# Giving every product with the transposed probabilities one stationary shape, 128 columns and 128 rows

## The chip, the cores and the metric

The kernel runs on one core of a Trainium2 chip. Its time is the device time of one launch in microseconds; three runs of the kernel before took 1256.52, 1258.52 and 1259.30 us, so the median is 1258.52. A profile is one further execution. The engines are TensorE (PE in the profile; its weight loads are a row of their own, PEld), VectorE (DVE), ScalarE (ACT), GpSimd (POOL), and SyncE (SP), whose queue issues all DMAs of this kernel.

## The reference

For 8 batches and 8 heads of 576 positions with 64 features, causal attention with a decay bias is computed, and its output goes through a feed-forward network (FFN) with an ELU:

```python
scores = scale * np.matmul(q, k.transpose(0, 1, 3, 2))
cum = np.cumsum(np.maximum(s, 0.0), axis=-1)
bias = -(cum[:, :, :, None] - cum[:, :, None, :])
scores = np.where(causal, -1000000000.0, scores + np.minimum(bias, 0.0))
attn = np.exp(scores - np.max(scores, axis=-1, keepdims=True))
attn = attn / (np.sum(attn, axis=-1, keepdims=True) + 1e-09)
out = np.matmul(attn, v)
# then, with x the 4608 x 512 matrix of all heads' outputs:
h = x @ w_in                                   # 512 x 2048
g = np.where(h > 0.0, h, np.exp(np.minimum(h, 0.0)) - 1.0)
y = g @ w_out                                  # 2048 x 512
```

All inputs and the output are float32.

## The kernel before

**Units.** Attention is worked through in 96 units, three for each of the 8 x 4 pairs of heads: one "pair" unit for the first 64 queries of both heads (`h is None`), and one unit for each head (`h` 0 and 1) with the other 512 queries. Each unit loads its operands (`prepare`), makes scores, softmax and scaled probabilities (`scoring`), and multiplies them with the values (`weighing`). The steps of one unit's weighing are interleaved with the scoring of the next.

**Two ways of arithmetic.** The first 24 units are "native": f32 operands, probabilities turned on TensorE (line 848) and copied out of PSUM into a tile `pc` (`split_pt`). In the units behind them a head's probabilities are split into an f16 high and low part (`halved`) and turned by transposing DMAs into a tile `T` (line 751). There are 48 such units. Their values are split too: three parts, each the upper 16 bits of a float32 word, lie in the tile `vs` as `[128, 5, 3, 64]`: five blocks of 128 keys, three parts, 64 features. `values` loads the tile and makes parts 1 and 2 by subtraction on POOL or DVE (line 660).

**The products.** For each key block `kb` of a head's unit `keys` (line 836) issues, into one PSUM bank `av`, a product of the first two parts side by side (128 stationary columns) with the high half of the probabilities, one of the third part (64 columns) with the high half, and one of the first two parts with the low half. The moving operand has 512, 448, 320 and 192 columns for blocks 0 to 3. The last block has 64 keys; its high and low halves share the 128 rows, so there are two products, the third part's with 64 rows and 64 columns. That makes 14 products for a unit, all of line 815. `halves` then adds the upper and the lower 64 rows of the result together.

**Buffers.** `vs` has two places, taken in turn by all three kinds of unit. `pc` has two places of 512 words, used by native head units and by the pair units. `T` has two places (`N_T`), one of which first holds the decay sums (`aux`, line 381).

**The FFN.** It runs in 12 chunks of 384 rows of x. A chunk has 16 steps `f`: 12 products of line 955 into `h`, the ELU on ACT, DVE and POOL, and 9 products of line 979 into `o`. Attention's outputs reach it through DRAM (`x_dram`).

**What sets the order.** Every operation is recorded with its engine (or several to choose from), a duration assumed by hand, its priority and the tiles it reads and writes. `Plan.issue` then places them greedily: of all operations that are ready and have a buffer, the one with the earliest start goes next, and the order on each engine is fixed so. A product with the transposed probabilities is assumed to take 0.4525 ns per moving column, whatever its stationary shape. A change in a buffer's number of places therefore may move instructions anywhere in the program.

Of the kernel before, what the change touches and what calls it, by code (L numbers as in the profile page):

```python
# [9 lines left out]
F32 = mybir.dt.float32  # L10
F32R = mybir.dt.float32r
# [6 lines left out]
P = 128  # L18
# [222 lines left out]
def pe4(n):  # L241

    return 4 * pe(n)
# [36 lines left out]
def kernel(  # L280
# [91 lines left out]
    k2 = [plan.buf(const, [P, S], F32R, f"k2_{k}") for k in range(2)]  # L372

    WM = S - P
    maskw = plan.buf(const, [P, WM], BF16, "maskw")
    masks = plan.buf(const, [P, 2, HB], BF16, "masks")

# [26 lines left out]
    def ones():  # L404

        for q, k in ((q2s, k2s), *zip(q2, k2)):
            def rows(q=q, k=k):
                pool.memset(q.v[HB:].bitcast(F32), 1.0)
                pool.memset(k.v[HB:].bitcast(F32), 0.0)

            op(-8, [("Pool", 700.0, rows)], [], [(q, "ones"), (k, ("aux", 0)), (k, ("aux", 1))])

    def mask_tiles():
        def whole():
# [129 lines left out]
    def prepare(u):  # L544

        b, j, h, prio = u.b, u.j, u.h, u.prio
        dt = F32 if u.native else F32R
        direct = u.native and (b, j) == (0, 0)
        u.vs = plan.buf(sb, [P, NQ + 1, 3, D], F32R if h is None and not u.native else F32,
                        f"vs_{u.tag}", tag="vs", bufs=2)  # L550
        if h is None:
            w, n, m = P, 2 * HB, 1
            u.qs = plan.buf(sb, [P, NQ * P], dt, f"qs_{u.tag}", tag="qs", bufs=2)
            u.kh = plan.buf(sb, [P, 2, HB], dt, f"khs_{u.tag}", tag="khs")
            u.q2, u.k2 = q2s, k2s
            heads = slice(2 * j, 2 * j + 2)

            def q_src():
                return qT[b, j, :, :P]

            def k_src():
                return kT[b, :, heads, :HB]

            def v_src():
                return vb[b, j, :, 0:1]

            def aux_src(m):
                h0 = b * H + 2 * j
                if direct:
                    return aux.v[h0 : h0 + 2, 0, :HB]  # L570
                return aux_dram.v[h0 : h0 + 2, m, :HB]

            def q_view(t):
                return t

            def k_view(t):
                return t.rearrange("p (h t) -> p h t", h=2)

            def k_own(t, rows):
                return t.v[rows]  # L580
        else:
            w, n, m = P * NQ, S, 1 + NQ
            u.qs = plan.buf(sb, [P, NQ * P], dt, f"qs_{u.tag}", tag="qs", bufs=2)
            spare = u.native and u.turn
            u.kh = plan.buf(sb, [P, S], dt, f"kh_{u.tag}", tag="st" if spare else "kh",
                            bufs=N_ST if spare else N_K)
            u.q2, u.k2 = q2[u.turn], k2[u.turn]
            hh = 2 * j + h

            def q_src():  # L590
                own = qT[b, j, :, P:].rearrange("p (i h t) -> p i h t", h=2, t=P)
                return own[:, :, h]

            def k_src():
                return kT[b, :, hh, :n]

            def v_src():
                return vb[b, j, :, 1:].rearrange("p (i h) d -> p i h d", h=2)[:, :m, h]

            def aux_src(m):  # L600
                h0 = b * H + hh
                return aux.v[h0 : h0 + 1, 0, :n] if direct else aux_dram.v[h0 : h0 + 1, m, :n]

            def q_view(t):
                return t.rearrange("p (i t) -> p i t", t=P)

            def k_view(t):
                return t

            def k_own(t, rows):  # L610
                return t.v[rows, :n]
        if u.native:

            load(prio, lambda: k_own(u.kh, slice(0, HB)), lambda: k_src()[:HB], [],
                 [(u.kh, "k")], HB * n * 4)
            at = slice(HB, HB + 1)
            op(prio, [("Pool", pool_1(w), lambda: pool.memset(u.qs.v[at, :w], 1.0))], [], [(u.qs, "ones")])
            load(prio, lambda: k_own(u.kh, at), lambda: aux_src(0),
                 [(aux, 0) if direct else (aux_dram, 0)], [(u.kh, "aux")], n * 4)
            load(prio, lambda: q_view(u.qs.v[:HB, :w]), lambda: q_src()[:HB], [],  # L620
                 [(u.qs, "q")], HB * w * 4)
            values(u, prio, v_src, m)
            return
        st = st_buf(f"stk_{u.tag}")
        load(prio, lambda: k_view(st.v[:, :n]), k_src, [], [st], P * n * 4)
        for m_ in range(2):
            at = slice(HB + 32 * m_, HB + 32 * m_ + 1)
            load(prio, lambda m_=m_, at=at: k_own(u.k2, at).bitcast(F32), lambda m_=m_: aux_src(1 + m_),
                 [(aux_dram, 1 + m_)], [(u.k2, ("aux", m_))], n * 4)
        sq = st_buf(f"stq_{u.tag}")  # L630
        load(prio, lambda: q_view(sq.v[:, :w]), q_src, [], [sq], P * w * 4)
        rounded(prio, w, lambda: u.qs.v[:, :w], lambda: sq.v[:, :w], [sq], [(u.qs, 0)])
        load(prio, lambda: u.q2.v[:HB, :w].bitcast(F32),
             lambda: u.qs.v[:HB, :w].bitcast(F32), [(u.qs, 0)], [(u.q2, "q")], HB * w * 4)
        rounded(prio, n, lambda: k_own(u.kh, slice(0, P)), lambda: k_view(st.v[:, :n]), [st], [u.kh])
        rest(prio, w, lambda: u.qs.v[HB:, :w], lambda: sq.v[HB:, :w],
             lambda: u.qs.v[HB:, :w].bitcast(F32), [sq, (u.qs, 0)], [(u.qs, 1)])
        rest(prio, n, lambda: k_own(u.k2, slice(0, HB)), lambda: k_view(st.v[:HB, :n]),
             lambda: k_own(u.kh, slice(0, HB)).bitcast(F32), [st, u.kh], [(u.k2, "kl")])
        if h is not None:  # L640
            values(u, prio, v_src, m)
            return
        sv = st_buf(f"stv_{u.tag}")

        def v3():
            return sv.v[:, :D].rearrange("p (n d) -> p n d", d=D)

        load(prio, v3, v_src, [], [sv], P * D * 4)
        rounded(prio, D, lambda: u.vs.v[:, :1, 0], v3, [sv], [u.vs])
        rest(prio, D, lambda: u.vs.v[:, :1, 1], v3,  # L650
             lambda: u.vs.v[:, :1, 0].bitcast(F32), [sv], [u.vs])
# [98 lines left out]
            ], [sm, (pt, "pad"), (t16, high)], [(t16, low), (pt, "data")])  # L750
        turned_load(prio, units[i], lambda: u.pt.v[:, (i + 1) % NQ :: NQ][:, : units[i]], lambda: t16.v, [t16], [(u.pt, i)])

    def split_pt(prio, tag, native, tr, w, t0=0, rows=P):
        pc = plan.buf(sb, [P, 512], F32 if native else F32R, f"pc_{tag}", tag="pc", bufs=2)
        psum_copy(prio, w, lambda: pc.v[:rows, :w], lambda: tr.v[:rows, t0 : t0 + w], [tr], [(pc, 0)])
        if native:
            return [(pc, 0)]
        op(prio, [("DVE", dve_p(w), lambda: dve.tensor_tensor(
            pc.v[:, 256 : 256 + w], tr.v[:, t0 : t0 + w], pc.v[:, :w].bitcast(F32), ALU.subtract))],
           [tr, (pc, 0)], [(pc, 1)])  # L760
        return [(pc, 0), (pc, 1)]

# [44 lines left out]
    def weighing(u):  # L807
# [11 lines left out]
        if u.h is None:  # L819
            def pair():  # L820
# [5 lines left out]
                products(pe4(P) if u.whole else pe(P), [  # L826
                    ([pc, u.vs], lambda pc=pc, m=m: (
                        u.vs.v.rearrange("p n a d -> p n (a d)")[:, 0, :rows],
                        pc[0].v[:, 256 * m : 256 * m + P]), rows)
                    for m, pc in enumerate(pieces)], slice(P), True, True)  # L830
                for h in range(2):
                    halves(prio, u.whole, 1.0, h, HB, u.x_part((h, 0)), 0, av, h * HB)
# [3 lines left out]
        def keys(kb):  # L836
# [3 lines left out]
            if u.whole:  # L840
# [3 lines left out]
                def turned():  # L844

                    ks = slice(kb * P, kb * P + rows)
                    for n, i in enumerate(range(i0, NQ)):
                        pe_.transpose(tr.v[:rows, n * P : (n + 1) * P], u.pp[i].v[:, ks], ident)

                op(prio, [("PE", 111.0 * (NQ - i0), turned)], [u.pp[i] for i in range(i0, NQ)], [tr])  # L850
                pc, = split_pt(prio, f"{u.tag}_{kb}", True, tr, c, HB * half, rows)
                products(pe4(c), [([pc, u.vs], lambda: (u.vs.v[:rows, kb, 0], pc[0].v[:rows, :c]), HB)],
                         dst, kb == 0, kb == NQ)
            else:

                i0 = max(kb - 1, 0)

                def part(m, rows):
                    if kb == NQ:
                        return u.pt.v[:rows, 0, P - c :]  # L860
                    end = (1 + (2 * kb + m + 1) * NQ) * P
                    return u.pt.v.rearrange("p u q -> p (u q)")[:rows, end - c : end]

                def two():
                    return upper(u.vs.v.rearrange("p n a d -> p n (a d)"))[:, kb, : 2 * D]

                def third(rows):
                    return upper(u.vs.v)[:rows, kb, 2]

                used = [(u.pt, i) for i in range(i0, NQ)]  # L870
                two_parts, three_parts = [(u.vs, 0), (u.vs, 1)], [(u.vs, 2)]
                rows = HB if kb == NQ else P
                pairs = [(used + two_parts, lambda m=m: (two(), part(m, P)), P)
                         for m in range(1 + (kb < NQ))]
                pairs.insert(1 - kb // NQ, (used + three_parts, lambda: (third(rows), part(0, rows)), HB))
                products(pe(c), pairs, dst, kb == 0, kb == NQ)
            if kb == NQ:
                halves(prio, u.whole, 1.0 if u.whole else 1.0 / UP, u.h, P * NQ,
# [211 lines left out]
```

## Time and profile before

| | us |
|---|---|
| median of three runs | 1258.52 |
| the profiled execution | 1260.03 |
| its span, first to last instruction | 1258.1 |
| PE busy | 1207.2 |
| POOL busy | 820.5 |
| DVE busy | 728.2 |
| ACT busy | 656.5 |
| granted TensorE clock, mean | 0.989 of full |

A row of the profile that names a line and an engine tells the operation, then what it writes and reads (`av<-T,vs`); for a PE row, `128*64` is the stationary operand's rows and columns and `128x512 f16` the moving operand. Matmuls are pipelined, so the durations of neighbours overlap, and the distance between two starts tells what one of them costs. In the views of waits, a row reads: engine and line that waited, `<-` whom it waited for, us in total, times, longest.

### The profile page before, as it was taken

Reading aid. Unit: us, or ns where it says so; the run is one execution under the profiler, and the core shown is the slowest. Engines: PE = TensorE matmul, PEld = TensorE weight load, DVE = VectorE, ACT = ScalarE, POOL = GpSimd, SP = SyncE. Lnnn points to the kernel's source line nnn. Section 1 sums busy time; section 2 is a strip of 40 time slices with the busy share of each in tenths; the row PEclk is TensorE's granted clock in tenths of the full one; section 3 lists DMA queues with packets and bytes.
Section 4 is the critical chain, followed back from the end, with each engine's and each line's share of the span. In section 5 each row is a group of like instructions: output and inputs, shape, how many; then the busy total and the mean of one; then the engine's idle time right before and its main releaser. Section 6 shows DMA issues by size and latency. Waiting matters only on the chain.

```text
span 1258.1 us, 19717 instructions
## 1 busy us (share of the span) xinstructions
PE 1207.2 (96%) x5888; PEld 935.4 (74%) x5888; DVE 728.2 (58%) x1849; ACT 656.5 (52%) x1607; POOL 820.5 (65%) x1055
## 2 busy tenths in 40 slices
PE   7999999899999999999999999999989999999998
PEld 4455567777778877777778767778777776988886
DVE  7867779845575555576576665566565555222221
ACT  5767766545555544565565554465555555232322
POOL 6766658757776777787787686777777676232321
PEclk9979999999999999999999999999999999999999
DMA  5645445554554555564565564554464554010100
GB/s 149 174 139 157 126 124 139 132 148 106 124 141 109 112 151 117 116 153 114 120 164 123 111 170 109 115 142 108 115 157 104 124 141 93 10 51 1 38 1 26
DMA packets 307367, 143.23 MB, mean 114 GB/s; under 512 B 233678, under 2 KB 283854, under 8 KB 307260
## 3 DMA queue, kind: packets, MB, share of 16 engines
q1 hardware_dynamic: 307260, 141.97, 46.2%
q8 instruction: 47, 0.77, 0.3%
q14 instruction: 60, 0.49, 0.1%
HBM read 73.04 MB, written 19.32 MB: 73 GB/s over the span
## 4 chain that ended last, share of the span: by engine, by line
PE 42%; DVE 5%; POOL 3%; issue 2%; ACT 1%; DMA 1%; POOLq 0%; DVEq 0%; ACTq 0%
PE o L979 16%; PE h L955 16%; PE av L815 7%; PE sc L686 2%; DVE g L964 1%; DVE p L689 1%; DVE vs L351 1%; POOL p L733 1%; DVE g L966 1%; POOL gl L352 1%; POOL p L734 1%; DVE p L747 1%; POOL p L739 0%; ACT g L963 0%; DMA stk<-in_kT_dram 0%
## 5 line engine op out<-in xcount | busy, mean ns | idle before, releaser
L352 POOL TENSOR_TENSOR gl<-g,gh 128x384 fp32r<-128x384 f32 x183 | 191.0, 1044 | 196.5 <-ACT gh L342 168.4
L955 PE MATMUL h<-xh,wi_h 128*128 128x384 f32 x768 | 267.5, 348 | 10.9 <-DVE g L966 10.8
L955 PE MATMUL h<-xl,wi_h 128*128 128x384 f32 x768 | 260.6, 339 | 0.9 <-POOL xl L352 0.8
L955 PE MATMUL h<-xh,wi_l 128*128 128x384 f32 x768 | 260.2, 339 | 0.0
L964 DVE TENSOR_SCALAR g<-g 128x384 f32<-128x384 f32 x192 | 98.9, 515 | 234.8 <-ACT g L963 234.6
L979 PE MATMUL o<-wo_h,gh 128*128 128x512 f32 x576 | 231.6, 402 | 0.6 <-POOL gh L340 0.4
L979 PE MATMUL o<-wo_h,gl 128*128 128x512 f32 x576 | 229.0, 397 | 1.7 <-POOL gl L352 1.7
L979 PE MATMUL o<-wo_l,gh 128*128 128x512 f32 x576 | 228.2, 396 | 0.0
L694 ACT ACTIVATE p<-p,mn 128x192 f32<-128x192 f32 (+3 forms) x256 | 156.9, 613 | 70.6 <-DVE mn L689 69.0
L963 ACT ACTIVATE g<-h 128x384 f32<-128x384 f32 x192 | 93.8, 488 | 172.0 <-PE h L955 123.5
L689 DVE CUSTOM_DVE_ANT_0 p<-sc,maskw 128x192 f32<-128x192 f32 (+3 forms) x256 | 119.4, 477 | 83.6 <-PE sc L686 73.9
L955 PEld LDWEIGHTS h<-xh,wi_h 128*128 128x128 f32 x768 | 146.2, 190 | 24.7 <-DVE g L966 16.0
L815 PE MATMUL av<-T,vs 128*128 128x512 f16 (+9 forms) x672 | 155.0, 315 | 0.1
L342 ACT ACTIVATE gh<-g 128x384 fp32r<-128x384 f32 x176 | 92.1, 523 | 120.3 <-DVE g L966 118.7
L955 PEld LDWEIGHTS h<-xl,wi_h 128*128 128x128 f32 x768 | 146.1, 190 | 10.4 <-POOL xl L352 3.0
L686 PE MATMUL sc<-kh,qs 128*128 128x288 f32 (+7 forms) x400 | 135.2, 390 | 16.9 <-DVE mn L689 16.1
L955 PEld LDWEIGHTS h<-xh,wi_l 128*128 128x128 f32 x768 | 145.9, 190 | 0.0
L815 PEld LDWEIGHTS <-vs 128*128 128x128 bf16 (+2 forms) x672 | 56.1, 101 | 104.2 <-issue 84.2
L979 PEld LDWEIGHTS o<-wo_h,gl 128*128 128x128 f32 x576 | 108.3, 188 | 31.0 <-POOL gl L352 6.1
L734 POOL TENSOR_TENSOR p<-p,p 128x512 f16<-128x512 f32 (+3 forms) x121 | 115.0, 951 | 10.1
L979 PEld LDWEIGHTS o<-wo_h,gh 128*128 128x128 f32 x576 | 108.9, 189 | 15.8 <-ACT gh L342 1.0
L979 PEld LDWEIGHTS o<-wo_l,gh 128*128 128x128 f32 x576 | 108.6, 188 | 14.4
(125 smaller groups left out, 1897.3 us busy)
## 6 DMA issues: line engine op xcount, KB each, us to landing
stk<-in_kT_dram SPq DMA_DIRECT2D x48, 288.0 KB
stq<-in_qT_dram SPq DMA_DIRECT2D x48, 256.0 KB
vs<-in_vb_dram SPq DMA_DIRECT2D x64, 160.0 KB
x_dram<-x SPq DMA_DIRECT2D x32, 288.0 KB
w_i<-in_w_in_dram SPq DMA_DIRECT2D x32, 256.0 KB
w_o<-in_w_out_dram SPq DMA_DIRECT2D x32, 256.0 KB
out_dram<-ost SPq DMA_DIRECT2D x32, 256.0 KB
xc<-x_dram SPq DMA_DIRECT2D x32, 192.0 KB
```

The costliest lines, as they stand in the source:

```text
L342: lambda: act.activation(dst(), src(), AF.Copy, scale=sign)),
L351: ("DVE", dve_2(n), lambda: dve.tensor_tensor(dst(), src(), hi(), ALU.subtract)),
L352: ("Pool", pool_2(n), lambda: pool.tensor_tensor(dst(), src(), hi(), ALU.subtract)),
L686: pe_.matmul(view(sc.v[:, :cw]), l, r, start=n == 0, stop=n == len(pairs) - 1)
L689: op(prio, [("DVE", 84 + dve_p(cw), lambda i=i, sc=sc: dve.tensor_tensor_reduce(pt.v[:, i * cw : (i + 1) * cw], sc.v[:, :cw], mv(i * cw, c ...
L694: op(prio, [("ACT", 480 + w / 1.2, lambda: act.activation(pt.v[:, :w], pt.v[:, :w], AF.Exp, bias=mn.v[:, n - 1 : n], scale=-1.0, accum_out ...
L734: pool.tensor_tensor(part(t16, 1), own(part), part(t16, 0), ALU.subtract)
L815: op(prio, [("PE", cost, lambda m=m, operands=operands, rows=rows: pe_.matmul(av.v[:rows, dst], *operands(), start=first and m == 0, stop= ...
L955: pe_.matmul(hp.v[:, :TC], w.v[:, c, fs], xx.v[:, c, :TC], start=(c == 0 and m == 0), stop=(c == NCB - 1 and m == 2),)
L963: op(side, [("ACT", act_c(TC), lambda: act.activation(g.v[:, :TC], hp.v[:, :TC], AF.Exp))], [hp], [g])
L964: op(side, [("DVE", dve_1(TC), lambda: dve.tensor_scalar(g.v[:, :TC], g.v[:, :TC], 1.0, -1.0, ALU.min, ALU.add))], [], [g])
L979: pe_.matmul(acc[i].v, g.v[:, tb], w.v[:, f], start=(f == 0 and m == 0), stop=(f == NF - 1 and m == 2),)
```

## The change

The value tiles of the head units become two fixed tiles, one for each head turn, with a fourth group of 64 columns that is zeroed once at the start. The third part is then multiplied together with the zeros beside it: 128 stationary columns, and 128 rows in the last block too (there the third part's copy in the lower rows is multiplied with the low half of the probabilities, a product that was left out before). The pair unit gets a small value tile of its own with one place. The pieces of turned probabilities (`pc`) are cut to the width they need; those of native head units move to the places of tile `T`, and those of pair units keep one place of the old kind.

```diff
+    vs = [plan.buf(const, [P, NQ + 1, 4, D], F32, f"vs_{k}") for k in range(2)]
...
+        for v in vs:
+            op(0, [("Pool", 450.0, lambda v=v: pool.memset(v.v[:, :, 3], 0.0))], [], [(v, "zeros")])
...
-        u.vs = plan.buf(sb, [P, NQ + 1, 3, D], F32R if h is None and not u.native else F32,
-                        f"vs_{u.tag}", tag="vs", bufs=2)
         if h is None:
             w, n, m = P, 2 * HB, 1
+            u.vs = plan.buf(sb, [P, 1, 2, D], dt, f"vs_{u.tag}", tag="vs0")
...
         else:
             w, n, m = P * NQ, S, 1 + NQ
+            u.vs = vs[u.turn]
...
-    def split_pt(prio, tag, native, tr, w, t0=0, rows=P):
-        pc = plan.buf(sb, [P, 512], F32 if native else F32R, f"pc_{tag}", tag="pc", bufs=2)
+    def split_pt(prio, tag, native, tr, w, t0=0, rows=P, home=("pc", 1)):
+        pc = plan.buf(sb, [P, 2, w], F32 if native else F32R, f"pc_{tag}", tag=home[0], bufs=home[1])
...
-                pc, = split_pt(prio, f"{u.tag}_{kb}", True, tr, c, HB * half, rows)
-                products(pe4(c), [([pc, u.vs], lambda: (u.vs.v[:rows, kb, 0], pc[0].v[:rows, :c]), HB)],
+                pc, = split_pt(prio, f"{u.tag}_{kb}", True, tr, c, HB * half, rows, ("T", N_T))
+                products(pe4(c), [([pc, (u.vs, 0)], lambda: (u.vs.v[:rows, kb, 0], pc[0].v[:rows, 0]), HB)],
                          dst, kb == 0, kb == NQ)
...
-                def third(rows):
-                    return upper(u.vs.v)[:rows, kb, 2]
+                def third():
+
+                    return upper(u.vs.v.rearrange("p n a d -> p n (a d)"))[:, kb, 2 * D :]
...
-                two_parts, three_parts = [(u.vs, 0), (u.vs, 1)], [(u.vs, 2)]
-                rows = HB if kb == NQ else P
-                pairs = [(used + two_parts, lambda m=m: (two(), part(m, P)), P)
+                two_parts, three_parts = [(u.vs, 0), (u.vs, 1)], [(u.vs, 2), (u.vs, "zeros")]
+                pairs = [(used + two_parts, lambda m=m: (two(), part(m)), P)
                          for m in range(1 + (kb < NQ))]
-                pairs.insert(1 - kb // NQ, (used + three_parts, lambda: (third(rows), part(0, rows)), HB))
+                pairs.insert(1 - kb // NQ, (used + three_parts, lambda: (third(), part(0)), P))
                 products(pe(c), pairs, dst, kb == 0, kb == NQ)
```

**The products on PE.** First, TensorE's order at the end of the products of one head's unit (batch 4, pair 1, head 0; blocks 3 and 4). The last number of a row is the size of the result, partitions by columns. Before:

```order
L815 MATMUL av_4_1_0_6370<-T_4_1_0_6254,vs_4_1_0_6087 128x192
L815 LDWEIGHTS vs_4_1_0_6087
L815 MATMUL av_4_1_0_6370<-T_4_1_0_6254,vs_4_1_0_6087 64x192
L815 LDWEIGHTS vs_4_1_0_6087
L815 MATMUL av_4_1_0_6370<-T_4_1_0_6254,vs_4_1_0_6087 128x192
L815 LDWEIGHTS vs_4_1_0_6087
L815 MATMUL av_4_1_0_6370<-T_4_1_0_6254,vs_4_1_0_6087 64x64
L815 LDWEIGHTS vs_4_1_0_6087
L815 MATMUL av_4_1_0_6370<-T_4_1_0_6254,vs_4_1_0_6087 128x64
```

Now:

```order
L819 MATMUL av_4_1_0_6162<-T_4_1_0_6055,vs_0_117 128x192
L819 LDWEIGHTS vs_0_117
L819 MATMUL av_4_1_0_6162<-T_4_1_0_6055,vs_0_117 128x192
L819 LDWEIGHTS vs_0_117
L819 MATMUL av_4_1_0_6162<-T_4_1_0_6055,vs_0_117 128x192
L819 LDWEIGHTS vs_0_117
L819 MATMUL av_4_1_0_6162<-T_4_1_0_6055,vs_0_117 128x64
L819 LDWEIGHTS vs_0_117
L819 MATMUL av_4_1_0_6162<-T_4_1_0_6055,vs_0_117 128x64
```

The number and order of the products stay; the narrow ones among them are as wide as their neighbours.

**The last unit among the FFN's products.** Second, TensorE's order at the products of the last unit (batch 7, pair 3, head 1). In `o_9_1`, 9 is the chunk and 1 the block of rows; in `gh_9_4`, 4 is the step. Before:

```order
L979 MATMUL o_9_1_11869<-wo_h_287,gh_9_4_12030 128x512
L979 MATMUL o_9_1_11869<-wo_l_295,gh_9_4_12030 128x512
L979 MATMUL o_9_1_11869<-wo_h_287,gl_9_4_12035 128x512
L815 LDWEIGHTS vs_7_3_1_11813
L815 MATMUL av_7_3_1_12056<-T_7_3_1_11967,vs_7_3_1_11813 128x512
```

Now:

```order
L983 MATMUL o_8_1_10873<-wo_h_252,gh_8_14_11749 128x512
L983 MATMUL o_8_1_10873<-wo_l_288,gh_8_14_11749 128x512
L983 MATMUL o_8_1_10873<-wo_h_252,gl_8_14_11758 128x512
L819 LDWEIGHTS vs_1_120
L819 MATMUL av_7_3_1_11780<-T_7_3_1_11704,vs_1_120 128x512
```

With 16 steps to a chunk, attention ends six steps of the FFN earlier in PE's order.

**The load of the values on SP.** Third, SP's queue where the values of batch 4, pair 1, head 0 are loaded; `T_4_0_1` is the transposed probabilities of the unit two before it. Before:

```order
L333 DMA_TRANSPOSE T_4_0_1_5973<-p16_4_0_1_3_5964 128x9x128
L328 DMA stk_4_1_1_6032<-in_kT_dram 128x576
L328 DMA q2_0_85<-qs_4_1_0_6050 64x512
L328 DMA stq_4_1_1_6068<-in_qT_dram 128x4x128
L328 DMA vs_4_1_0_6087<-in_vb_dram 128x5x64
```

Now:

```order
L333 DMA_TRANSPOSE T_4_0_1_5802<-p16_4_0_1_1_5769 128x6x128
L328 DMA q2_0_85<-qs_4_1_0_5839 64x512
L328 DMA vs_0_117<-in_vb_dram 128x5x64
L328 DMA stk_4_1_1_5860<-in_kT_dram 128x576
L333 DMA_TRANSPOSE T_4_0_1_5802<-p16_4_0_1_3_5811 128x9x128
```

The load stood behind the last transpose of that unit and now stands ahead of it.

More of the change, by code (lines that the diff above doesn't have):

```diff
@@ L751, in halved @@
         turned_load(prio, units[i], lambda: u.pt.v[:, (i + 1) % NQ :: NQ][:, : units[i]], lambda: t16.v, [t16], [(u.pt, i)])
-    def split_pt(prio, tag, native, tr, w, t0=0, rows=P):
-        pc = plan.buf(sb, [P, 512], F32 if native else F32R, f"pc_{tag}", tag="pc", bufs=2)
-        psum_copy(prio, w, lambda: pc.v[:rows, :w], lambda: tr.v[:rows, t0 : t0 + w], [tr], [(pc, 0)])
+    def split_pt(prio, tag, native, tr, w, t0=0, rows=P, home=("pc", 1)):
+        pc = plan.buf(sb, [P, 2, w], F32 if native else F32R, f"pc_{tag}", tag=home[0], bufs=home[1])
+        psum_copy(prio, w, lambda: pc.v[:rows, 0], lambda: tr.v[:rows, t0 : t0 + w], [tr], [(pc, 0)])
         if native:
@@ L758, in split_pt @@
         op(prio, [("DVE", dve_p(w), lambda: dve.tensor_tensor(
-            pc.v[:, 256 : 256 + w], tr.v[:, t0 : t0 + w], pc.v[:, :w].bitcast(F32), ALU.subtract))],
+            pc.v[:, 1], tr.v[:, t0 : t0 + w], pc.v[:, 0].bitcast(F32), ALU.subtract))],
            [tr, (pc, 0)], [(pc, 1)])
@@ L828, in pair @@
                         u.vs.v.rearrange("p n a d -> p n (a d)")[:, 0, :rows],
-                        pc[0].v[:, 256 * m : 256 * m + P]), rows)
+                        pc[0].v[:, m]), rows)
                     for m, pc in enumerate(pieces)], slice(P), True, True)
@@ L856, in keys, with part @@
                 i0 = max(kb - 1, 0)
-                def part(m, rows):
+                def part(m):
                     if kb == NQ:
-                        return u.pt.v[:rows, 0, P - c :]
+                        return u.pt.v[:, 0, P - c :]
                     end = (1 + (2 * kb + m + 1) * NQ) * P
-                    return u.pt.v.rearrange("p u q -> p (u q)")[:rows, end - c : end]
+                    return u.pt.v.rearrange("p u q -> p (u q)")[:, end - c : end]
                 def two():
                     return upper(u.vs.v.rearrange("p n a d -> p n (a d)"))[:, kb, : 2 * D]
-                def third(rows):
-                    return upper(u.vs.v)[:rows, kb, 2]
+                def third():
+                    return upper(u.vs.v.rearrange("p n a d -> p n (a d)"))[:, kb, 2 * D :]
                 used = [(u.pt, i) for i in range(i0, NQ)]
-                two_parts, three_parts = [(u.vs, 0), (u.vs, 1)], [(u.vs, 2)]
-                rows = HB if kb == NQ else P
-                pairs = [(used + two_parts, lambda m=m: (two(), part(m, P)), P)
+                two_parts, three_parts = [(u.vs, 0), (u.vs, 1)], [(u.vs, 2), (u.vs, "zeros")]
+                pairs = [(used + two_parts, lambda m=m: (two(), part(m)), P)
                          for m in range(1 + (kb < NQ))]
-                pairs.insert(1 - kb // NQ, (used + three_parts, lambda: (third(rows), part(0, rows)), HB))
+                pairs.insert(1 - kb // NQ, (used + three_parts, lambda: (third(), part(0)), P))
                 products(pe(c), pairs, dst, kb == 0, kb == NQ)
```

## The prediction

> **What bounds the kernel now.** I read the busy line of the page first, then the busy times by stage, then the waits of TensorE, and only then the rows of the products that the diff touches.
>
> ```profile
> span 1258.1 us, 19717 instructions
> ...
> PE 1207.2 (96%) x5888; PEld 935.4 (74%) x5888; DVE 728.2 (58%) x1849; ACT 656.5 (52%) x1607; POOL 820.5 (65%) x1055
> ```
>
> TensorE (PE) is busy for 96% of the span and the next engine for 65%. A busy PE may still be stalled inside, so this alone decides nothing. By stage (columns: stretch, its length, busy us and count of PE, PEld, DVE, ACT, POOL, then granted clock, DMA share, GB/s):
>
> ```profile
> 0.00:200.00 200.00, 185.05 (x772) 112.06 (x773) 149.47 (x449) 132.94 (x361) 131.58 (x249) 0.96 0.52 146
> 200.00:300.00 100.00, 92.28 (x453) 73.13 (x451) 75.19 (x169) 58.83 (x144) 72.42 (x84) 0.98 0.53 129
> 200.00:1070.00 870.00, 842.31 (x4226) 663.54 (x4225) 538.30 (x1316) 473.89 (x1149) 635.88 (x753) 0.99 0.54 127
> 1070.00:1258.00 188.00, 179.81 (x893) 159.82 (x891) 40.43 (x85) 49.71 (x98) 53.02 (x54) 1.00 0.07 21
> ```
>
> The first stage is attention with whole f32 products, which the diff leaves as they are but for a buffer. From 200 to 1070 us the 48 units with transposed f16 probabilities run, filled with FFN products; there PE idles 870.0 - 842.3 = 27.7 us, POOL is 73% busy and DVE 62%. The last 188 us are FFN alone. What PE waits for in the middle stage (us in total, times, longest):
>
> ```profile
> PE sc L686 <- DVE mn L689: 15.4, 19, 2.2
> PE h L955 <- DVE g L966: 8.6, 9, 2.2
> ```
>
> So nearly all of the middle stage is PE's own stream. Now one unit's 14 products in order of time (start us, duration us); durations overlap, so what counts is the distance from start to start:
>
> ```profile
> 602.03 0.39 PE L815 MATMUL av<-T,vs 128*128 128x512 f16 x1
> 602.35 0.40 PE L815 MATMUL av<-T,vs 128*64 128x512 f16 x1
> 602.69 0.39 PE L815 MATMUL av<-T,vs 128*128 128x512 f16 x1
> 602.91 0.35 PE L815 MATMUL av<-T,vs 128*128 128x448 f16 x1
> 603.20 0.38 PE L815 MATMUL av<-T,vs 128*64 128x448 f16 x1
> 603.51 0.36 PE L815 MATMUL av<-T,vs 128*128 128x448 f16 x1
> 603.71 0.30 PE L815 MATMUL av<-T,vs 128*128 128x320 f16 x1
> 603.94 0.32 PE L815 MATMUL av<-T,vs 128*64 128x320 f16 x1
> 604.19 0.31 PE L815 MATMUL av<-T,vs 128*128 128x320 f16 x1
> 604.34 0.25 PE L815 MATMUL av<-T,vs 128*128 128x192 f16 x1
> 604.52 0.27 PE L815 MATMUL av<-T,vs 128*64 128x192 f16 x1
> 604.72 0.26 PE L815 MATMUL av<-T,vs 128*128 128x192 f16 x1
> 604.91 0.21 PE L815 MATMUL av<-T,vs 64*64 64x64 f16 x1
> 605.05 0.20 PE L815 MATMUL av<-T,vs 128*128 128x64 f16 x1
> 605.09 0.34 PE L686 MATMUL sc<-kh,qs 128*128 128x192 f32 x1
> ```
>
> Where a 128*128 product is followed by another, the distance is 0.22 us after 512 columns, 0.20 after 448, 0.15 after 320, 0.04 after 64. Where the stationary shape changes, it is 0.32 and 0.34 at 512, 0.29 and 0.31 at 448, 0.23 and 0.25 at 320: about 0.1 us more at each of the ten changes of a unit. It isn't the accumulation into one bank, which the unchanged pairs share. The weight loads tell the same (busy us, mean ns | idle us before):
>
> ```profile
> L815 PEld LDWEIGHTS <-vs 128*128 128x128 bf16 x432 | 30.6, 98 | 44.4 <-issue 28.9 <-DVE g L964 1.1 <-DMA k<-aux_dram 0.3
> ...
> L815 PEld LDWEIGHTS <-vs 128*64 128x64 bf16 x192 | 20.5, 107 | 55.3 <-issue 55.3
> ```
>
> A narrow load stands 55.3 / 192 = 0.29 us behind nothing that the profile names, where the wide ones average 0.10: it isn't pulled ahead into the product before it. The Trainium skill, TensorEngine Tiling (Array Packing), Key Properties, says that changing the tiling mode drains TensorE; the trace agrees, with the tenth of a microsecond above.
>
> **The change part by part.** *Third parts 128 wide, 128 rows.* All 14 products of a unit get one stationary shape, so all ten changes go. New distances: 3 x 0.22 + 3 x 0.20 + 3 x 0.15, then 192 columns, which no unchanged pair shows: 0.15 less the step of 0.05 that 128 columns make from 448 to 320, so 0.10, three times, and 2 x 0.04. Sum 0.66 + 0.60 + 0.45 + 0.30 + 0.08 = 2.09 us. Before it is 605.09 - 602.03 = 3.06, and the chain of waits has the same at other units:
>
> ```profile
> 591.20 3.07 PE av L815 x14
> ...
> 1066.55 3.07 PE av L815 x14
> ```
>
> The gain is 0.97 us a unit; with x192 narrow loads in fours, 48 units: **-46.6 us**, all on PE. Upper bound of the new cost: if no load were hidden, each short product would stand for its 98 ns load; that changes only the two of 64 columns, 2 x 0.06 x 48 = 5.8 us. I take 0, because behind the last product of 64 columns an f32 product follows after 0.04. The extra 64 zero columns stream nothing: distance goes with the moving columns. A rule speaks against the change: the Trainium skill, TensorE: Matmul & The Clock Gate, LDWEIGHTS (loading the stationary operand), has load time go with stationary columns, by its formula an estimated 53 ns for 64 and 107 for 128, or 12.8 us over 240 loads were they exposed. The rows above have 107 ns for 64 columns and 98 for 128, and the measurement decides.
>
> *Zero fills.* Two POOL memsets of 128x320 at the start. The nearest row:
>
> ```profile
> L443 POOL MEMSET p<- 128x64 f32 x27 | 3.8, 156 | 3.7 <-PE tr L848 3.4
> ```
>
> Five times that at most, 0.8 us each, 200 us before a transposed unit reads the zeros: 0, and 1.6 if POOL's start is late.
>
> *Homes of the buffers.* The value tiles were two, taken in turn by three kinds of unit, so a load waited for the products of the unit just before; now each head turn has its own, and the order puts the load ahead of transposes that it stood behind. Pieces of probabilities in the first stage go to tile T's two places, of which one holds the decay sums for a while; the pair unit has one place for two. The waits at stake (the third is for a pieces buffer):
>
> ```profile
> SPq L328 <- PE av L815: 44.3, 23, 4.0
> ...
> POOL vs L352 <- DMA vs<-in_vb_dram: 18.6, 8, 4.1
> ...
> ACT pc L358 <- PE av L815: 5.0, 8, 1.0
> ```
>
> Neither of the engines in these rows bounds, so I take 0. Bounds: the third doubles (+5) or the second vanishes with half its time reaching PE (-9).
>
> *The planner's order.* It moves attention ahead of the FFN: the last unit's products stood in chunk 9 behind step 4, now in chunk 8 behind step 14, six steps earlier. A step is 12 and 9 products:
>
> ```profile
> 1074.59 2.08 PE h L955 x12
> 1076.67 2.10 PE o L979 x9
> ```
>
> So 6 x 4.18 = 25 us of FFN move behind attention. PE's sum stays, but the middle stage shrinks to 870 - 46.6 - 25 = 798 us with DVE's 538 in it: 67% in place of 62%. From 200 to 300 us DVE is at 75% and PE idles 7.7%, against 3.2% over the stage; a third of the way gives 4.9% of 798 = 39 us, +11. Against it, ACT waits for these very products, and each ends a microsecond sooner:
>
> ```profile
> ACT x L893 <- PE av L815: 70.7, 31, 4.4
> ```
>
> 31 such waits less 0.97 are 30 us that ACT gets back. Between 0 and +11 I take **+4**. One more chunk boundary falls clear of attention; such a one leaves PE idle 1.10 us (an earlier gap of 0.27 beside it):
>
> ```profile
> 1120.17 0.44 PE L955 MATMUL h<-xh,wi_h 128*128 128x384 f32 x1 [1.10 <-DVE g L966]
> ```
>
> **+1**. Sum on the profiled execution, 1260.0 us (span 1258.1 and 1.9 around it): 1260.0 - 46.6 + 4 + 1 = 1218.4. The median of the runs, 1258.5, lies 1.5 lower: **1217 us**. The first stage adds an uncertainty of both signs, since it has half-clock stretches that its stalls may bring or spare:
>
> ```profile
> 60.00:67.00 7.00, 6.59 (x14) 2.27 (x14) 6.83 (x18) 4.41 (x13) 5.88 (x10) 0.51 0.84 236
> 75.00:88.00 13.00, 12.30 (x39) 9.20 (x39) 9.23 (x33) 9.15 (x23) 7.70 (x14) 0.61 0.48 140
> ```
>
> 0.49 x 7 + 0.39 x 13 = 8.5 us. **Rivals.** *More is given back:* vector work paces the denser stage, up to half of the gain, 1258.5 - 23 = 1235. For it is the stretch from 200 to 300 us, against it the 27.7 us of idle time over 870.
>
> *More is gained:* values arrive earlier (-9), and the half-clock stretches go (-8.5 at most): about 1200.
>
> *Slower:* the units are paced by the chain from scores over DVE, ACT, POOL and the transposing DMAs, one unit each 870 / 48 = 18.1 us. Then what PE saves is idle, attention still ends near 1070 us, and the 25 us of FFN moved behind it lengthen the tail: 1258.5 + 25 = 1284. It decides once PE's idle time in the stage reaches 27.7 + 46.6 + 25 = 99 us; the two waits above give no sign of it.
>
> *The change doesn't do what it says:* the tenth of a microsecond belongs to something else in the third part, and stays: 1258 with the reordering's few us either way. The unchanged pairs speak against it.
>
> **How the numbers follow.** A measurement of this kernel can tell 0.2%, 2.5 us. Forecast, 1206 to 1226: 0.60. More given back, 1226 to 1248: 0.18. More gained, below 1206: 0.13. No effect of the shape: 0.05, of which 0.03 within 0.2% and 0.01 on each side. Slower by pace: 0.04. Faster 0.60 + 0.18 + 0.13 + 0.01 = 0.92, same 0.03, slower 0.05. The range of 1200 to 1238 takes in half of each neighbour.
>
> **What would show it.** One unit's 14 products take 2.1 us from first to last start and the next; the narrow loads' group is gone, and the idle time behind "issue" with it; PE's idle time between 200 us and the end of attention stays under 45 us; attention ends near 1005 us, and the tail is some 25 us longer. I am wrong if the distances within a unit stay near 0.3 us at 512 columns (the shape wasn't the cause), or if they shrink while attention still ends past 1040 us (another engine paces it).

## The result, and the profile after

The changed kernel takes 1220.45 us (median of four runs, 1218.62 to 1224.11), the kernel before 1257.52 us in the same comparison. The ratio is 0.971, with a 95% interval from 0.968 to 0.974: 37 us less, where 41 were forecast. The profiled execution was the longest of the four, 1224.11 us.

The busy line of the page of after, and the busy times by stage, cut at the first and the last product with transposed probabilities (columns as in the prediction):

```profile
span 1222.3 us, 19691 instructions
...
PE 1155.8 (95%) x5888; PEld 937.7 (77%) x5888; DVE 745.5 (61%) x1864; ACT 636.1 (52%) x1569; POOL 830.1 (68%) x1072
```

```profile
216.00:1008.00 792.00, 754.91 (x4021) 632.53 (x4021) 537.11 (x1281) 437.06 (x1070) 620.18 (x739) 0.99 0.59 135
1008.00:1222.00 214.00, 205.94 (x1023) 182.95 (x1020) 45.95 (x97) 58.08 (x114) 62.09 (x64) 1.00 0.08 25
```

Attention ends at 1008 us in place of 1069, and the FFN's tail has grown from 189 us to 214, the 25 us of FFN that the new order puts behind attention. In the middle stage PE is idle for 792.0 - 754.9 = 37 us.

One unit's products after, in order of time (start us, duration us), with the product of the FFN that follows the fourteenth:

```profile
557.50 0.39 PE L819 MATMUL av<-T,vs 128*128 128x512 f16 x1
557.72 0.38 PE L819 MATMUL av<-T,vs 128*128 128x512 f16 x1
557.94 0.38 PE L819 MATMUL av<-T,vs 128*128 128x512 f16 x1
558.16 0.35 PE L819 MATMUL av<-T,vs 128*128 128x448 f16 x1
558.35 0.35 PE L819 MATMUL av<-T,vs 128*128 128x448 f16 x1
558.53 0.35 PE L819 MATMUL av<-T,vs 128*128 128x448 f16 x1
...
559.44 0.48 PE L983 MATMUL o<-wo_h,gh 128*128 128x512 f32 x1
```

From 557.50 to 559.44 are 1.94 us, where the kernel before took 3.07. The distances from start to start, as medians over all units, are 216, 189, 136, 82 and 28 ns behind 512, 448, 320, 192 and 64 columns. Between 64 and 512 columns that is (216 - 28) / 448 = 0.42 ns for each moving column, and 1 to 2 ns on top of it. The weight loads form one group, and the idle time that nothing explains is down from 55 us before the narrow loads alone to 12 in all:

```profile
L819 PEld LDWEIGHTS <-vs 128*128 128x128 bf16 x672 | 59.8, 98 | 50.4 <-issue 11.5 <-DMA k2s<-aux_dram 1.8 <-DVE g L968 0.6
```

What PE's weight loads wait for in the middle stage of after (us in total, times, longest). `sc` are the banks of the scores, which DVE empties in the step that makes `mn`; `gl` and `xl` are the low parts of the FFN's activations and of its input, which POOL makes:

```profile
PEld sc L690 <- DVE mn L693: 27.6, 29, 4.1
PEld o L983 <- POOL gl L352: 12.2, 23, 1.5
...
PEld h L959 <- POOL xl L352: 6.6, 7, 2.6
```

### The profile page after: what moved, and what is told of

It reads as the page before. It is cut to its first block, busy times and chain, and to the rows that moved or that the text cites. A ratio compares the mean times of both kernels' runs of the same rounds, so it can differ in the third digit from the quotient of the medians.

```text
span 1222.3 us, 19691 instructions
## 1 busy us (share of the span) xinstructions
PE 1155.8 (95%) x5888; PEld 937.7 (77%) x5888; DVE 745.5 (61%) x1864; ACT 636.1 (52%) x1569; POOL 830.1 (68%) x1072
## 5 line engine op out<-in xcount | busy, mean ns | idle before, releaser
L968 DVE TENSOR_SCALAR g<-g 128x384 f32<-128x384 f32 x192 | 103.9, 541 | 244.9 <-ACT g L967 243.9
L342 ACT ACTIVATE gh<-g 128x384 fp32r<-128x384 f32 x167 | 87.4, 523 | 122.9 <-DVE g L970 122.0
L751 DVE SCALAR_TENSOR_TENSOR p<-p,sm,p 128x512 f16<-128x512 f32 (+3 forms) x127 | 117.4, 942 | 15.5 <-POOL p L743 12.5
L738 POOL TENSOR_TENSOR p<-p,p 128x512 f16<-128x512 f32 (+3 forms) x113 | 110.8, 980 | 9.4
L690 PEld LDWEIGHTS sc<-kh,qs 128*128 128x128 f32 (+1 forms) x400 | 75.3, 198 | 49.9 <-DVE mn L693 32.2
```

The costliest lines, as they stand in the source:

```text
L342: lambda: act.activation(dst(), src(), AF.Copy, scale=sign)),
L690: pe_.matmul(view(sc.v[:, :cw]), l, r, start=n == 0, stop=n == len(pairs) - 1)
L738: pool.tensor_tensor(part(t16, 1), own(part), part(t16, 0), ALU.subtract)
L751: ("DVE", dve_2(n), lambda part=part: dve.scalar_tensor_tensor(part(t16, 1), own(part), sm.v[:, r], part(t16, 0), ALU.mult, ALU.subtract)),
L968: op(side, [("DVE", dve_1(TC), lambda: dve.tensor_scalar(g.v[:, :TC], g.v[:, :TC], 1.0, -1.0, ALU.min, ALU.add))], [], [g])
```

## Experiments

Where an experiment leaves the order of all engines as it was, its trace can be laid beside the other instruction by instruction: for each of PE's 5888 products, the distance to the next start in the one is subtracted from that in the other. The sums over four parts of the span say where time went, and they are used below. "Products" are the 48 units' products, "between" is all else from the first of them to the last. The sums are of one execution each. The kernel before was run again beside every experiment, with medians of 1256.1 to 1257.5 us, and "less than the kernel before" goes by the median of the same comparison.

| from, to (same order) | first stage | products | between | tail | all |
|---|---|---|---|---|---|
| before, wide_old | -1.8 | -54.1 | +11.5 | 0.0 | -44.4 |
| before, grouped_old | -1.6 | -37.7 | +3.5 | 0.0 | -35.8 |
| narrow_new, after | +0.6 | -55.0 | +14.2 | 0.0 | -40.2 |
| rows64, after | +0.5 | -10.1 | +4.8 | +0.1 | -4.7 |
| before, before_lightgl | -2.7 | 0.0 | -18.0 | -0.6 | -21.3 |
| wide_old, wide_lightgl | -1.6 | -0.1 | -22.6 | -0.7 | -25.0 |
| before_lightgl, wide_lightgl | -0.7 | -54.2 | +7.0 | 0.0 | -47.9 |

### The shape alone, in the old order

```diff
-                def third(rows):
-                    return upper(u.vs.v)[:rows, kb, 2]
+                def third():
+                    return upper(u.vs.v.rearrange("p n a d -> p n (a d)"))[:, kb, D : 3 * D]
...
-                pairs.insert(1 - kb // NQ, (used + three_parts, lambda: (third(rows), part(0, rows)), HB))
+                pairs.insert(1 - kb // NQ, (used + three_parts, lambda: (third(), part(0, P)), P))
```

> The kernel before with one thing changed: the third part's product takes parts 1 and 2 of the values as 128 stationary columns and all 128 rows. It has no zeros, so part 1 is added once too often: the values are not the reference's, the work is. Buffers and the order on every engine are those of before. By the distances of the profile after (0.216, 0.189, 0.136, 0.082 and 0.028 us) a unit's products take 1.93 us in place of 3.07, 54.7 us less over 48 units. Theory P (what was given back goes to waits that appear whenever PE gets faster, in any order): 1258 - 55 + 18 = 1221. Theory O (the 18 us were lost to the new order and buffers): about 1205. If the shape were not the cause: 1258.

Measured: 1216.0 us, ratio 0.967 (0.964 to 0.970), 40.5 us less. The shape is the cause: nothing else differs, and the products take 54.1 us less. Neither theory of the loss has its number: 11.5 us come back as waits between the products in the same order, where P had 18 and O none. The waits of the weight loads in the middle stage, first of the kernel before, then of wide_old:

```profile
PEld L815 <- issue: 84.2, 326, 0.4
PEld sc L686 <- DVE mn L689: 22.3, 24, 2.7
...
PEld o L979 <- POOL gl L352: 4.7, 11, 0.8
PEld h L955 <- POOL xl L352: 1.8, 5, 0.6
```

```profile
PEld sc L686 <- DVE mn L689: 22.4, 24, 2.8
PEld o L979 <- POOL gl L352: 13.5, 24, 1.0
...
PEld L815 <- issue: 9.0, 37, 0.9
PEld h L955 <- POOL xl L352: 5.8, 7, 1.9
```

The unexplained time is gone, the waits for DVE stay, and waits for POOL's `gl` and `xl` go from 6.5 us to 19.3. Laid side by side, 5.1 of the 11.5 us stand ahead of products with `gl`, 3.0 ahead of products with `xl`; the rest is spread.

### The order and the buffers alone

```diff
-                    return upper(u.vs.v.rearrange("p n a d -> p n (a d)"))[:, kb, 2 * D :]
+                    return upper(u.vs.v)[:rows, kb, 2]
...
-                pairs.insert(1 - kb // NQ, (used + three_parts, lambda: (third(), part(0)), P))
+                pairs.insert(1 - kb // NQ, (used + three_parts, lambda: (third(), part(0, rows)), HB))
```

> The changed kernel with the third part's product narrow again (64 columns, 64 rows in the last block); buffers, zero fills and the order on every engine stay those of the change. The ten changes of shape come back, so PE has 54.7 us more than after. Theory P: the new order is worth nothing by itself, 1258 within 4. Theory O: 1220 + 55 = 1275. If the new order helped: under 1250.

Measured: 1263.8 us, ratio 1.0049 (1.0032 to 1.0066): the new order and the new buffers cost 7.3 us by themselves by the medians, 4 to 8 us by the interval. Between the two theories, again: P had 0, O 18. With wide products the same comparison, after against wide_old, gives 1220.4 - 1216.0 = 4.4 us, but their intervals (0.968 to 0.974, 0.964 to 0.970) overlap, so there the difference isn't clear.

### Is a narrow product slow, or the change of shape?

```diff
-                pairs.insert(1 - kb // NQ, (used + three_parts, lambda: (third(rows), part(0, rows)), HB))
-                products(pe(c), pairs, dst, kb == 0, kb == NQ)
+                late.append((pe(c), [(used + three_parts, lambda: (third(rows), part(0, rows)), HB)], dst))
+                if kb == NQ:
+                    for cost, one, to in late:
+                        products(cost, one, to, False, False)
+                products(pe(c), pairs, dst, kb == 0, kb == NQ)
```

> The kernel before with the five narrow products of a unit issued one behind the other, ahead of the last wide product; their shapes, their number and everything else stay. Of ten changes of shape three are left (wide to 64 columns, 128 to 64 rows, back to wide). Theory S (the change of shape costs about 0.11 us each): a unit takes 1.93 + 3 x 0.11 = 2.26 us, 0.81 x 48 = 39 us less on PE, and the time is 1219 if nothing is given back, 1232 if a third is. Rival (a narrow product is slow in itself, whatever its neighbours): 3.07 us a unit, 1258.

Measured: 1226.3 us, ratio 0.976 (0.973 to 0.978), 30.2 us less with no product wider than before. A unit takes 2.28 us, 2.26 were expected. The narrow products of one unit, and what follows (the row marked x2 holds the products of 320 and of 192 columns):

```profile
577.14 0.41 PE L815 MATMUL av<-T,vs 128*64 128x512 f16 x1
577.38 0.35 PE L815 MATMUL av<-T,vs 128*64 128x448 f16 x1
577.57 0.38 PE L815 MATMUL av<-T,vs 128*64 128x320 f16 x2
577.88 0.21 PE L815 MATMUL av<-T,vs 64*64 64x64 f16 x1
578.03 0.20 PE L815 MATMUL av<-T,vs 128*128 128x64 f16 x1
578.07 0.48 PE L984 MATMUL o<-wo_h,gh 128*128 128x512 f32 x1
```

Behind a narrow product with 448 columns the next narrow one starts after 0.19 us, as a wide one behind a wide one does in after; over all units the medians are 189 ns in both, and 136 in both at 320 columns. Between neighbours of one shape a narrow product costs what a wide one costs. It is the change that costs: 0.15 us lie between the 64*64 product and the wide one, where 64 columns of one shape take 0.03.

### Rows

```diff
-                    return upper(u.vs.v.rearrange("p n a d -> p n (a d)"))[:, kb, 2 * D :]
+                    return upper(u.vs.v.rearrange("p n a d -> p n (a d)"))[:rows, kb, 2 * D :]
```

> The changed kernel with 64 rows in the last block's third product (its 128 columns and all else stay): two changes of the number of rows come back for each unit. Theory S for rows too: 2 x 0.11 x 48 = 10 us on PE, 1226 to 1231. Rival (only the number of columns matters): 1220 within 3.

Measured: 1228.4 us, ratio 0.977 (0.975 to 0.980), 8 us more than after; the two intervals don't overlap. The number of rows counts as the number of columns does:

```profile
563.22 0.25 PE L819 MATMUL av<-T,vs 128*128 128x192 f16 x1
563.40 0.20 PE L819 MATMUL av<-T,vs 64*128 64x64 f16 x1
563.53 0.20 PE L819 MATMUL av<-T,vs 128*128 128x64 f16 x1
563.57 0.48 PE L985 MATMUL o<-wo_h,gh 128*128 128x512 f32 x1
```

0.18 us in place of 0.08, 0.13 in place of 0.03, and one hundredth more behind it. The change's 128 rows in the last block, zero gain by the old account of work, are worth 10.1 us on PE. Of the 4.8 us that after has more between the products, 3.5 are one wait, which is taken up further below.

### Less vector work for the values

```diff
-            rest(prio, m * D, lambda i=i: u.vs.v[:, :m, i + 1], lambda i=i: u.vs.v[:, :m, i],
-                 lambda i=i: upper(u.vs.v)[:, :m, i], [(u.vs, i)], [(u.vs, i + 1)])
+            rest(prio, m * D, lambda i=i: u.vs.v[:, :1, i + 1], lambda i=i: u.vs.v[:, :1, i],
+                 lambda i=i: upper(u.vs.v)[:, :1, i], [(u.vs, i)], [(u.vs, i + 1)])
```

The fixed tiles' parts 1 and 2 are zeroed at the start together with the zeros. The same edit was then made with narrow products.

> The changed kernel in its own order on every engine, but the two subtractions that split a unit's values work on one key block of five (64 columns in place of 320); the parts of the other blocks stay zero, so the split is left out there. That takes some 0.5 us from each of 96 instructions, about 50 us of POOL and DVE work. Theory P (PE waits for vector engines that have little room left): some of the 14 us come back, 1210 to 1216. Rival (PE's waits are the latency of the chain score, DVE, ACT, not the engines' load): 1220 within 3.

> Both edits together: the changed kernel with narrow third products (PE slower by 55 us) and with the light split of the values (50 us less vector work, one key block of five split). Order on every engine as in the change. The light split took 7 us where PE was fast (1220.4 to 1213.1). Theory P (PE waits for vector engines only because its own stream got shorter): with the longer stream the same relief is worth less, 0 to 3 us, so 1261 to 1264. Rival (these waits stand on the path whatever PE does): the same 7 us, 1256 to 1257.

Measured: 1213.1 us, ratio 0.965 (0.964 to 0.967), 7.3 less than after; and with narrow products 1255.5 us, ratio 0.9998 (0.9985 to 1.0010), 8.3 less than narrow_new. The relief on the busy lines is 43 us (POOL 830.1 to 800.8, DVE 745.5 to 731.7). It is worth about the same whether PE's stream is long or short. Theory P as it was put, that PE waits for vector engines only because its own stream got shorter, falls: these waits are there with the long stream too.

### Less work on POOL for the FFN

```diff
-            ("Pool", pool_2(n), lambda: pool.tensor_tensor(dst(), src(), hi(), ALU.subtract)),
+            ("Pool", pool_2(n), lambda: pool.tensor_tensor(dst(), src(), hi(), ALU.subtract)
+             if cheap is None else pool.tensor_scalar(dst(), src(), cheap, 1.0, ALU.mult, ALU.mult)),
...
-            rest(side, TC, lambda: gl.v[:, :TC], lambda: g.v[:, :TC], lambda: gh.v[:, :TC].bitcast(F32), [g, gh], [gl])
+            rest(side, TC, lambda: gl.v[:, :TC], lambda: g.v[:, :TC], lambda: gh.v[:, :TC].bitcast(F32), [g, gh], [gl],
+                 cheap=2.0**-13)
```

> wide_old with one more edit: POOL makes the low part of the FFN's activations (gl, 183 instructions of 1.04 us) by one multiplication of g in place of a subtraction of two operands, some 0.52 us each; it leaves the low part out, so its output isn't the reference's. Order on every engine as before. In wide_old PE's instructions between the units' products take 11.5 us more than before, 5.1 of it ahead of products with gl and 3.0 ahead of products with xl. Theory P2 (with the shorter stream POOL comes late with gl and xl): 5 to 9 us of that come back, 1207 to 1211. Rival (the waits are for something that POOL doesn't set): 1216 within 2.

> The kernel before with the same cheaper gl on POOL, and nothing else. Theory P2: with the long stream POOL was hardly late, so 0 to 3 us, 1254 to 1257. Rival (gl stands on the path whatever PE does): as much as in wide_old.

Measured: 1193.2 us, ratio 0.949 (0.946 to 0.952), 22.8 less than wide_old; and 1239.6 us, ratio 0.986 (0.984 to 0.989), 16.8 less than the kernel before. Both effects are larger than expected, and in the kernel before the rival comes near: most of the relief is there whatever PE does. The difference between the two, 6.0 us by the medians, is about as large as their noise; between the products the two pairs of traces differ by 4.6 us, and that sits where theory P2 put it: ahead of products with `gl` 6.6 us go in wide_old and 1.9 in the kernel before. With the cheaper `gl` the change of shape gives back 7.0 us in place of 11.5, so some 4.5 of the 11.5 are POOL's lateness with `gl`. The group of `gl` in the kernel before and in before_lightgl:

```profile
L352 POOL TENSOR_TENSOR gl<-g,gh 128x384 fp32r<-128x384 f32 x183 | 191.0, 1044 | 196.5 <-ACT gh L342 168.4 <-issue 23.3 <-PE o L979 2.2
```

```profile
L353 POOL TENSOR_SCALAR gl<-g 128x384 fp32r<-128x384 f32 x183 | 100.1, 547 | 199.5 <-DVE g L967 183.7 <-PE o L981 4.7 <-PE h L956 1.9
```

The releasers in these rows show that the edit does more than halve the instruction. The subtraction reads `gh`, the multiplication doesn't: in the kernel before no `gl` starts before its `gh` has ended, here 92 of 192 do. So the two runs tell what a cheaper and earlier `gl` is worth. The waits of the weight loads in the middle stage, of before_lightgl and of wide_lightgl:

```profile
PEld L816 <- issue: 83.7, 323, 0.7
PEld sc L687 <- DVE mn L690: 13.1, 17, 2.2
...
PEld o L981 <- POOL gl L353: 0.7, 2, 0.4
```

```profile
PEld sc L687 <- DVE mn L690: 11.7, 17, 2.2
...
PEld h L956 <- POOL xl L352: 6.1, 7, 1.4
PEld o L981 <- POOL gl L353: 1.8, 5, 0.6
```

91 us less work on POOL take only 4.0 us from the waits for `gl` in the kernel before (4.7 to 0.7 us). What shrinks most is the wait of the scores for DVE, 22.3 to 13.1 us. DVE's instructions are the same 1849, but they run faster: DVE was busy for 728.2 us before and is for 701.5 here, while ACT's busy time stays (656.5 and 655.2).

```profile
PE 1195.4 (97%) x5888; PEld 932.5 (75%) x5888; DVE 701.5 (57%) x1849; ACT 655.2 (53%) x1607; POOL 729.9 (59%) x1055
```

One group of DVE's instructions, in the kernel before and in before_lightgl:

```profile
L747 DVE SCALAR_TENSOR_TENSOR p<-p,sm,p 128x256 f16<-128x256 f32 x24 | 22.8, 949 | 6.0 <-POOL p L739 4.0 <-DMA q2s<-qs_None 1.2 <-ACT p L743 0.6
```

```profile
L748 DVE SCALAR_TENSOR_TENSOR p<-p,sm,p 128x256 f16<-128x256 f32 x24 | 17.0, 708 | 5.0 <-POOL p L740 4.2 <-ACT p L744 0.6
```

Within the trace of the kernel before the same shows: DVE's first step on `g` (line 964, 192 times) takes 360 ns as a median where POOL is idle throughout and 546 ns where POOL works for more than half of it. The next step on `g` (line 966), which reads `h` from PSUM, takes 558 and 557 ns. So part of DVE's work is slower while POOL is at work, and less POOL work makes DVE faster too. How much of the 16.8 us comes that way, and how much through `gl` itself, was not separated.

### Three versions that compute everything

Wide products in the native units (an f32 product beside a part that is zero), then the planner told the new durations, then both:

```diff
-                products(pe4(c), [([pc, (u.vs, 0)], lambda: (u.vs.v[:rows, kb, 0], pc[0].v[:rows, 0]), HB)],
+                products(pe4(c), [([pc, (u.vs, 0), (u.vs, 1)], lambda: (
+                    u.vs.v.rearrange("p n a d -> p n (a d)")[:rows, kb, :P],
+                    pc[0].v[:rows, 0]), P)],
```

```diff
-                products(pe(c), pairs, dst, kb == 0, kb == NQ)
+                products(3 + c / 2.4, pairs, dst, kb == 0, kb == NQ)
```

> The changed kernel with the native units' products (f32, first stage) 128 columns wide as well: the part beside the values is zeroed, the last block keeps its 64 rows. Order on every engine as in the change. In the first stage after, 124 neighbours on PE differ in shape, and a product that a change follows takes 0.04 to 0.1 us more; some 60 of these go. Theory S: 3 to 6 us less, 1215 to 1218. Rival (the first stage is paced by other engines, or f32 products pay nothing for a change): 1220 within 2.

> The changed kernel with the planner told the duration that the products now have (3 ns and 1/2.4 ns a column, in place of 0.4525 ns a column and at least 111): a unit is planned with 1.9 us in place of 2.3. The order changes on all engines. If the 18 us were lost because the planner had the old durations: 1210 to 1215. If they were lost to the load of the other engines: 1220 within 6, as any other order.

> The changed kernel with wide products in the native units too and with the planner told the products' new duration; it computes all of it. If the two add up (3 us and 0): 1217. If this order happens to fit better or worse: 1210 to 1224.

Measured: 1217.1 us, ratio 0.9685 (0.967 to 0.970); 1221.0 us, ratio 0.971 (0.968 to 0.973); 1218.7 us, ratio 0.968 (0.964 to 0.971). The first stage of native_wide is 4.1 us shorter than after's in the same order (the first transposed product starts at 212.4 us in place of 216.5), as the changes of shape there let expect, and 3.2 us come back behind it in the profiled execution, the longest of its five. None of the three is clearly faster than the change: all intervals overlap its own. Telling the planner the new durations brought nothing in the one order that came of it.

One more number of the planner, since POOL's load had turned out to count:

```diff
-    BIAS = {"DVE": 3.0}
+    BIAS = {"DVE": 2.0}
```

> native_wide with one number of the planner changed: DVE's durations are weighed 2 times in place of 3 where an operation may go to several engines, so some 70 operations move from POOL to DVE and the order changes everywhere. It computes all of it. If POOL's load is what PE waits for most (a cheaper gl on POOL took 17 us from the kernel before and 23 from wide_old): 1205 to 1212. If DVE, already 61% busy and in the chain from scores to probabilities, gives it back: 1217 to 1230.

Measured: 1235.3 us, ratio 0.982 (0.979 to 0.985), 18 us slower than native_wide, from which it differs by this number alone.

```profile
PE 1150.9 (93%) x5888; PEld 951.4 (77%) x5888; DVE 828.0 (67%) x1954; ACT 623.7 (50%) x1549; POOL 763.8 (62%) x962
```

```profile
PE sc L690 <- DVE mn L693: 34.4, 25, 2.3
```

POOL's 69 us less become 84 us more on DVE, whose lateness with the score banks now holds PE for 34.4 us over the whole span (20.3 in native_wide). The order changes everywhere too, so that DVE's load alone costs the 18 us isn't shown; that moving this work from POOL to DVE doesn't pay here is.

## Why the prediction was right, and where its terms were off

**The likeliest case came, by a sum whose terms were off in opposite directions.** 1217 us were forecast, 1220.45 measured, and attention ended at 1008 us where 1005 was forecast. The mechanism was right: the changes of shape cost PE the tenth of a microsecond each, and some of the gain is given back. That the time came within 4 us is in part luck: 8 us too little on the products stand against some 13 too little on all that comes back (5 forecast, about 55 - 37 = 18 measured).

**The cause.** That the tenth of a microsecond belongs to the change of shape was read from neighbours in one trace; wide_old and grouped_old show it by taking the changes away in two ways. The rival by which it belonged to the third part itself, or to the accumulation, falls. The Trainium skill, TensorEngine Tiling (Array Packing), Key Properties, says that a change of the tiling mode drains TensorE, and a change of the tile alone doesn't. The traces agree with the first: the time is lost at the changes, and between two products of one narrow shape nothing is lost. No run here changes the tile alone.

**The first term was too small: -46.6 forecast, -54 to -55 measured.** The step that failed is "where a 128*128 product is followed by another, the distance is 0.22 us". Each such pair in the kernel before stood behind a change, and the start behind a change comes 12 ns late as well: 228 ns there, 216 in a row of equals. And the 0.10 us for 192 columns, carried on from those distances, is 0.082, which makes 0.05 of the 0.16 us by which a unit's 2.09 was too long (1.93 by these distances). A narrow product between wide ones costs about 93 + 121 + 12 = 226 ns: the change to it (176 ns at 192 columns where equals have 82), the change back (203 where equals have 82), and the start behind that (201 at 448 columns where equals have 189); at 320, 448 and 512 columns the sums are 226 to 227 too. Four such and the last block's make 1.13 us a unit. The Trainium skill, TensorE: Matmul & The Clock Gate, "Wait — 56ns, not 53.3ns?", has N / 2.4 GHz plus about 2.5 ns between two starts at full clock, an estimated 216 ns for 512 columns and 29 for 64; the trace of after agrees with 216 and 28. With the bound for exposed loads there was no loss: even 64 columns follow each other after 28 ns, under loads that last 98.

**The second term was too small too: +4 forecast for what is given back, +11.5 measured in the old order and +14.2 in the new.** The direction was right, and so was the size of PE's idle time after (37 us, under 45), but the mechanism was only partly seen. It was put down to DVE's share in a denser stage; the waits that grew are for POOL's `gl` and `xl`. For `gl` that is shown, by its relief, for some 4.5 us. What the rest is made of stays open: with the cheaper `gl` 4.6 of the 7.0 us stand ahead of products with `xl`, which no run made cheaper, and DVE is busy 7.0 us longer in wide_old than before with the same instructions (735.2 and 728.2). One wait of 3.7 us ahead of a score product stands in the profiled executions of after and native_wide, the longest of the runs of each, and not in those of narrow_new, rows64 or light_values, which have the same order; so the 14.2 holds some chance.

**The reading "nearly all of the middle stage is PE's own stream" was too simple.** In the kernel before, a cheaper and earlier `gl` took 18.0 us from what lies between the products. The prediction showed the waits of PE's products alone, in which `gl` and `xl` have 1.5 us; its weight loads wait 6.5 us for them, and 22.3 for the scores' banks.

**The homes of the buffers were put at 0 with bounds of -9 and +5, and the boundary at +1; narrow_new has +7.3 for buffers and order together.** Part of that belongs to the +4, which also covered the six steps of the FFN that leave the middle stage. The value load ahead of the transposes brought no visible gain. Which of the moved instructions cost the 7 us was not separated.

**The rivals.** "More is given back" holds in part, but its price was set against a gain that was itself too small. "Slower by pace" falls: attention ended 61 us earlier. "More gained" is not what happened in time, though the products alone gained more.

## What to carry to other kernels

Look for changes of the stationary shape, in columns or rows, between neighbouring matmuls: in this kernel each narrow bf16 product among wide ones cost 0.23 us more than one among equals, at 192 columns as at 512, and filling it up with zeros, or merely issuing the narrow ones one behind the other, took most of that away. Read what a product costs from rows of equals, not from pairs behind a disturbance. And a TensorE that is busy for 96% is no proof that nothing else counts: before trusting it, make one other engine's work cheaper and see, and look at whether a second engine got faster with it.

## What was not expected of the hardware

With TensorE busy for 96% of the span, 0.5 us less in each of 183 POOL instructions, which also started earlier, took 16.8 us from the kernel before (before_lightgl), and DVE's unchanged instructions ran 27 us shorter with it. The busy share of TensorE hides this, for the rows of matmuls overlap in the profile: its idle time in the middle stage, 26 us, fell to 16, while the distances between starts shrank by 18, and its busy time over the span fell from 1207.2 to 1195.4 us with the same products. Nor was it expected that a start behind a change of shape is followed by one that is 12 ns late as well, or that f32 products pay for a change too: in native_wide, 15 of the 16 transposes behind a now wide product of 448 columns start 94 to 112 ns sooner than behind the narrow one in after.
